# Six output buffers, a longer lag and kept-back product slots in the middle of a fused attention and two-layer kernel

## The chip, the cores and the metric

The kernel runs on one core of a Trainium2 chip. Times are device microseconds of one execution; a lower time is better. Each kernel is run several times, with the kernel before in the same rounds on the same chip. Faster or slower takes 2%.

## The reference

Attention of 4 batches x 8 heads x 768 positions x 64, where heads 0, 2 and 6 (the retrieval heads) see all earlier positions and the other five (the streaming heads) a window of 64 and the first four positions, the sinks; then a product with `w_in`, a leaky ReLU, and a product with `w_out`:

```python
scores = np.matmul(q, k.transpose(0, 1, 3, 2)) / sqrt(64)      # masked by head
a = softmax(scores)
x = np.matmul(a, v).transpose(0, 2, 1, 3).reshape(3072, 512)
h = x @ w_in                                                   # 512 x 2048
out = np.maximum(0.01 * h, h) @ w_out                          # 2048 x 512
```

## The kernel before

The 3072 rows are worked in eight chunks of 384. In the steady part TensorE works on three chunks at once: slots of the attention of chunk n+1, product slots (`in`) of chunk n, and sum slots (`out`) of chunk n-1, merged in program order. Every engine gets its instructions in that order; semaphores make them wait for one another. Heads are worked in four pairs, 0 to 3. Copying a result out of its PSUM bank is called its eviction; until then the next product into it waits (in the trace before, a `ph` eviction from 40.38 us ends at 40.87, and the weights of the next product start at 40.92). The kernel uses eight banks, two for each of four tags: `ph` (product), `psS` (scores, and transposes of the attention's result), `po` (values), `py` (sums).

```python
BANKS = {"ph": 2, "psS": 2, "po": 2, "py": 2}
...
k0, q0 = bf("k0", 3, H, D), bf("q0", 3, H, D)                  # memory of their own
f0 = {nm: rot.tile([128, DM], FP32, name="o", tag="o", bufs=3)... for nm in ("k", "q")}
...
def slots(self, order=range(H), lag=2):                        # one attention, in slots
    ...
    LAG, X = lag, 0 if self.cross else 3
    for t in range(len(units) + LAG + X):
        def slot(t=t):
            for p in range(4):
                if X and t == last[p] + LAG + X:
                    self.x_t(p, box[p], eng=self.xt_eng)       # transposes of pair p, into a psS bank
            if t < len(units):
                units[t][0]()                                  # scores into a psS bank, exp on ScalarE
            if 0 <= t - LAG < len(units):
                ... units[t - LAG][1]()                        # values, LAG slots later
                ... box[p] = self.finish(p)                    # reciprocal and scaling on VectorE
...
def in_slots(n, tags=("ph",)):       # 16 slots: 4 matmuls of 384 columns, eviction on ScalarE
...
            if hi == NG:             # end of a sum
                o = rot.tile([128, DM], FP32, name="o", tag="o", bufs=3)
                nc.vector.tensor_copy(o[:, 0 : c1 - c0], py[n][:, 0 : c1 - c0])
                nc.sync.dma_start(out=out[r0 : r0 + 128, c0:c1], in_=o[:, 0 : c1 - c0])
...
run(in_slots(1, ("ph",)))                                      # chunk 1's product, alone
...
run(merge(o0[10:] + o1[0:12], Attention(2).slots()))           # chunk 2's attention
run(spreads(3))
for n in range(2, NCH):
    ...
        extra = spreads(n + 2)                                 # key copies of chunk n+2, VectorE
    ...
        a = into(Attention(n + 1, cross=n > 2).slots(), extra)
    ms = merge(in_slots(n), outs)
    rest = ms[-9:] if a and n > 2 else []
    run(merge(ms[: len(ms) - len(rest)], a), rest)
```

The softmax here doesn't subtract the row's maximum and nothing guards it: scores larger than these inputs give would overflow.

## Time and profile before

| | before |
|---|---|
| median of three runs | 240.12 us (238.11 to 240.46) |
| span of the profiled run | 237.9 us |
| TensorE busy | 227.9 us, 96% |
| ScalarE / VectorE busy | 54% / 40% |

Shares of busy time do not say where time can be won, since a matmul's end in the profile is modelled: between 40 and 60 us TensorE shows 20.00 us busy of 20.00, with seven gaps of 0.09 us between starts in it (40.92 to 49.25 us). What is read below is when each matmul starts, against the start of the matmul before it plus the time that the columns of that earlier one take. The prediction shows the lines.

### The profile page before, as it was taken

What the parts mean: (1) busy time and instruction counts of PE and PEld (TensorE: products, weight loads), DVE (VectorE), ACT (ScalarE), POOL (GpSimd) and SP (SyncE); (2) the same over time, 40 slices, a digit from 0 to 9 for tenths busy, and PEclk for the clock granted to TensorE, in tenths of its full rate; (3) what the DMA queues carried; (4) which work ended last, traced back from release to release, by engine and by line L of the source; (5) the groups of instructions that cost most, each with busy time, mean ns of one, the idle gap of its engine ahead of it and who ended that gap; (6) DMA issues with size and microseconds to landing.
All of it is one profiled execution on the core that took longest, in us unless ns stands there. A gap on an engine that the chain in (4) does not pass through costs nothing.

```text
span 237.9 us, 5107 instructions
## 1 busy us (share of the span) xinstructions
PE 227.9 (96%) x2073; PEld 140.7 (59%) x2073; DVE 95.5 (40%) x281; ACT 128.4 (54%) x276; POOL 71.4 (30%) x87
## 2 busy tenths in 40 slices
PE   5889899999998999899999999999999999999995
PEld 3679666544665666466556565666556665555544
DVE  6587777105436345345512652144411441111112
ACT  4573875732663888664446543765556764333300
POOL 8975634035367087139002900000000000000000
PEclk9999999999999999999999999999999999999999
DMA  9999999999999999599929992930110211111012
GB/s 130 155 182 166 204 209 163 175 113 154 156 247 203 166 178 144 91 156 156 146 59 207 166 168 57 191 113 19 62 62 0 63 34 61 47 44 44 30 61 90
DMA packets 109480, 28.98 MB, mean 122 GB/s; under 512 B 101248, under 2 KB 105744, under 8 KB 109456
## 3 DMA queue, kind: packets, MB, share of 16 engines
q0 software_dynamic: 77088, 13.39, 74.2%
q1 hardware_dynamic: 31312, 15.00, 30.3%
q10 hardware_dynamic: 1056, 0.26, 0.5%
q8 instruction: 16, 0.26, 0.5%
q14 instruction: 8, 0.07, 0.1%
HBM read 27.30 MB, written 6.29 MB: 141 GB/s over the span
## 4 chain that ended last, share of the span: by engine, by line
PE 88%; DMA 4%; DVE 3%; ACT 3%; issue 1%; ACTq 0%; DVEq 0%
PE ph L553 32%; PE py L579 29%; PE po L294 6%; PE psS L325 5%; PE psS L579 3%; DMA out_dram<-o 3%; PE ph L566 2%; PE psS L360 2%; PE psS L305 2%; DMA o<-in_q_dram 2%; PE py L212 1%; ACT at L330 1%; PE psS L403 1%; PE po L510 1%; DVE xs L393 1%
## 5 line engine op out<-in xcount | busy, mean ns | idle before, releaser
L553 PE MATMUL ph<-xt,w_in_bf 128*128 128x384 bf16 x480 | 95.5, 325 | 0.0
L579 PE MATMUL py<-w_out_bf,g 128*128 128x512 bf16 (+1 forms) x352 | 91.0, 374 | 0.0
L555 ACT ACTIVATE g<-ph 128x384 bf16<-128x384 f32 x120 | 59.0, 492 | 57.5 <-PE ph L553 56.8
L553 PEld LDWEIGHTS <-w_in_bf 128*128 128x128 bf16 x480 | 43.7, 97 | 31.3 <-issue 1.3
L579 PEld LDWEIGHTS <-g 128*128 128x128 bf16 x416 | 35.7, 97 | 25.8
L330 ACT ACTIVATE at<-psS 128x384 bf16<-128x384 f32 x78 | 36.8, 490 | 15.5 <-PE psS L325 15.3
L585 DVE COPY o<-py 128x512 f32<-128x512 f32 (+1 forms) x22 | 14.9, 678 | 52.9 <-PE py L579 50.9
L112 POOL DMA_DIRECT2D kb<-in_k_dram x21 | 18.8, 908 | 38.3 <-DMA kd<-kb 37.8
L325 PE MATMUL psS<-qd,kt 128*128 128x384 bf16 (+2 forms) x90 | 22.9, 294 | 0.0
L117 POOL DMA_DIRECT2D va<-in_v_dram x24 | 21.3, 904 | 3.0 <-DMA w_out_bf<-in_moe_w_out_dram 1.5
L112 POOL DMA_DIRECT2D qb<-in_q_dram x21 | 18.7, 911 | 7.5 <-DMA w_in_bf<-in_moe_w_in_dram 3.2
L294 PE MATMUL po<-va,at 128*128 128x65 bf16 x228 | 19.4, 193 | 0.3 <-DVE at L333 0.3
L365 ACT ACTIVATE ats<-psS 128x384 bf16<-128x384 f32 x35 | 17.0, 490 | 4.4 <-PE psS L360 4.1
L369 DVE TENSOR_TENSOR ats<-ats,m_win 128x384 bf16<-128x384 bf16 x35 | 12.4, 358 | 16.3 <-ACT ats L365 16.2
L294 PEld LDWEIGHTS <-at 128*128 128x128 bf16 x234 | 15.1, 98 | 5.6 <-DVE at L333 0.7
L393 DVE TENSOR_TENSOR xs<-po,linv 128x384 bf16<-128x384 f32 x27 | 15.1, 558 | 0.9
L335 DVE TENSOR_TENSOR at<-at,m_caus 128x128 bf16<-128x128 bf16 x21 | 4.7, 226 | 24.9 <-ACT at L330 24.9
L360 PEld LDWEIGHTS <-kt 128*128 128x128 bf16 x210 | 10.8, 98 | 6.3 <-issue 0.4
L325 PEld LDWEIGHTS <-kt 128*128 128x128 bf16 x99 | 9.5, 97 | 7.6 <-issue 1.2
L294 PEld LDWEIGHTS <-ats 128*128 128x128 bf16 x210 | 10.1, 98 | 4.1 <-DVE ats L369 0.8
L233 DVE COPY kt<-kd 64x512 bf16<-64x512 bf16 x36 | 11.8, 326 | 0.6
L333 DVE TENSOR_TENSOR at<-at,m_caus 128x256 bf16<-128x256 bf16 x21 | 6.1, 293 | 14.6 <-ACT at L330 14.6
(139 smaller groups left out, 197.3 us busy)
## 6 DMA issues: line engine op xcount, KB each, us to landing
out_dram<-o SPq DMA_DIRECT2D x23, 256.0 KB, 2.3
va<-in_v_dram POOLq DMA_DIRECT2D x24, 128.0 KB, 7.5
kb<-in_k_dram POOLq DMA_DIRECT2D x21, 128.0 KB, 5.6
qb<-in_q_dram POOLq DMA_DIRECT2D x21, 128.0 KB, 5.9
w_in_bf<-in_moe_w_in_dram POOLq DMA_DIRECT2D x4, 512.0 KB, 10.1
w_out_bf<-in_moe_w_out_dram POOLq DMA_DIRECT2D x4, 512.0 KB, 12.7
vb<-va SPq DMA_DIRECT2D x8, 195.0 KB, 4.8
vb<-va SPq DMA_DIRECT2D x4, 130.0 KB, 3.1
```

The costliest lines, as they stand in the source:

```text
L112: nc.gpsimd.dma_start(out=t[:, g], in_=nat[nm][b, c, :, :, g])
L117: nc.gpsimd.dma_start(out=va[b][:, 3 * c + g, :, 0:D], in_=nat["v"][b, c, :, :, g])
L294: nc.tensor.matmul(o, lhsT=lhsT, rhs=rhs, start=first, stop=False, skip_group_check=True)
L325: nc.tensor.matmul(s[:, off : off + w], lhsT=kt[i][:, p, hh, 128 * kj : 128 * kj + 128], rhs=q_of(n, p, lo, CH), start=(j == 0), stop=(j = ...
L330: nc.scalar.activation(out=a[:, 0:off], in_=s[:, 0:off], func=ACTF.Exp, scale=SM)
L360: nc.tensor.matmul(s[:, 64 * m : 64 * m + 64], lhsT=kt[i][:, p, hh, k0 : k0 + 128], rhs=q_of(n, p, 64 * m, 64 * m + 64), start=(m == 0), s ...
L365: nc.scalar.activation(out=av_, in_=s[:, 0:CH].rearrange("p (j e f) -> p j e f", j=3, e=2), func=ACTF.Exp, scale=SM)
L393: nc.vector.tensor_tensor(xs[:], po[:, :, :, 0:D], linv.to_broadcast([128, 3, 2, D]), op=ALU.mult)
L553: nc.tensor.matmul(ph[:, 0:CH], lhsT=w_in_bf[:, g, 128 * t : 128 * t + 128], rhs=xts[n][:, g, :], start=(g == 0), stop=(g == KG - 1))
L555: nc.scalar.activation(out=gs[n][:, t, :], in_=ph[:, 0:CH], func=ACTF.Prelu, alpha=0.01)
L579: nc.tensor.matmul(py[n][:, 0 : c1 - c0], lhsT=gs[n][:, ng, 128 * tt : 128 * tt + 128], rhs=w_out_bf[:, ng, c0:c1], start=(ng == 0), stop= ...
L585: nc.vector.tensor_copy(o[:, 0 : c1 - c0], py[n][:, 0 : c1 - c0])
```

## The change

Its intent: the copy of a sum should not wait for an output transfer; the product that runs alone should borrow two idle banks; values should follow their scores three slots later; and the end of chunk 3's attention should have product slots to fill its waits, with the next key copies out of VectorE's way.

```diff
-    k0, q0 = bf("k0", 3, H, D), bf("q0", 3, H, D)
-    f0 = {... tag="o", bufs=3 ...}
+    k0 = rot.tile([128, 3, H, D], BF16, name="k0", tag="kd", bufs=2)
+    q0 = rot.tile([128, 3, H, D], BF16, name="q0", tag="qd", bufs=3)
+    f0 = {... tag="o", bufs=6 ...}
...
-                o = rot.tile([128, DM], FP32, name="o", tag="o", bufs=3)
+                o = rot.tile([128, DM], FP32, name="o", tag="o", bufs=6)
...
-    run(in_slots(1, ("ph",)))
+    run(in_slots(1, ("ph", "psS")))
...
-    run(merge(o0[10:] + o1[0:12], Attention(2).slots()))
+    run(merge(o0[10:] + o1[0:12], Attention(2).slots(lag=3)))
...
-            a = into(Attention(n + 1, cross=n > 2).slots(), extra)
+            a = Attention(n + 1, cross=n > 2).slots(lag=2 if n > 2 else 3)
+            a = into(a, extra) if n > 2 else a
...
+        if n == 2:
+            a, rest = a[:-3], [ms[-4], a[-3], ms[-3], a[-2], a[-1], ms[-2], ms[-1]] + extra
+            ms = ms[:-4] + rest
```

More of the change, by code (lines that the diff above doesn't have):

```diff
@@ L93 @@
     raw = {}
-    k0, q0 = bf("k0", 3, H, D), bf("q0", 3, H, D)
-    f0 = {nm: rot.tile([128, DM], FP32, name="o", tag="o", bufs=3).rearrange("p (h d) -> p h d", h=H) for nm in ("k", "q")}
+    k0 = rot.tile([128, 3, H, D], BF16, name="k0", tag="kd", bufs=2)
+    q0 = rot.tile([128, 3, H, D], BF16, name="q0", tag="qd", bufs=3)
+    f0 = {nm: rot.tile([128, DM], FP32, name="o", tag="o", bufs=6).rearrange("p (h d) -> p h d", h=H) for nm in ("k", "q")}
     def load_first(nm):
```

## The prediction

> **What bounds the kernel now.** I read the page first, then the waits, then the chain in order of time, and last the timeline of the stretch that the change touches (38 to 100 us).
>
> ```profile
> span 237.9 us, 5107 instructions
> PE 227.9 (96%) x2073; PEld 140.7 (59%) x2073; DVE 95.5 (40%) x281; ACT 128.4 (54%) x276; POOL 71.4 (30%) x87
> PE 88%; DMA 4%; DVE 3%; ACT 3%; issue 1%; ACTq 0%; DVEq 0%
> ```
>
> The chain in order of time has this line for the first product of chunk 1 (start, us, what):
>
> ```profile
> 38.30 11.76 PE ph L553 x68
> ```
>
> TensorE sets the end: 88% of the chain that ended last is its work. Only time in which TensorE could have started a matmul and did not is to be had. Its busy time does not show that, as ends are modelled; starts do. In the chain four 384-column matmuls take 0.65 us, 162 ns each. So I compare each matmul's start with the start before it plus its columns at 162 ns per 384 (30 ns for a 65-column one). Between 100 us and the last product this leaves nothing over 0.06 us but one 0.3 us gap at 170 us; 0 to 35 us has larger ones, which the change does not touch. What lies between 38 and 100 us is all that is on offer:
>
> 1. The chunk 1 first product, alone on TensorE: 68 matmuls at 162 ns are 11.02 us, the chain line has 11.76. The evictions show the pattern:
>
> ```profile
> 39.64 0.49 ACT L555 ACTIVATE g<-ph 128x384 bf16<-128x384 f32 x1 [0.16 <-PE ph L553]
> 40.38 0.49 ACT L555 ACTIVATE g<-ph 128x384 bf16<-128x384 f32 x1 [0.25 <-PE ph L553]
> ...
> 40.92 1.23 PEld L553 LDWEIGHTS <-w_in_bf 128*128 128x128 bf16 x8 [0.16 <-issue]
> 41.03 0.49 ACT L555 ACTIVATE g<-ph 128x384 bf16<-128x384 f32 x1 [0.16 <-PE ph L553]
> ```
>
> Evictions start 0.74 and 0.65 us apart in turn: two slots take 1.39 us where TensorE needs 1.30. The 40.38 eviction ends at 40.87, the next weights at 40.92: two ph banks are one too few. The stretch has seven such gaps of 0.09 us, 0.65 us in all.
>
> 2. Chunk 2's attention, 57 to 77 us:
>
> ```profile
> DVE o L585 <- DMA out_dram<-o: 1.6, 1, 1.6
> ```
>
> That was the line of the waits (who <- for whom: us, times, longest); in the timeline (start, us, what):
>
> ```profile
> 53.55 0.69 DVE L585 COPY o<-py 128x512 f32<-128x512 f32 x1 [10.55 <-PE py L579]
> ...
> 64.79 1.38 SPq L586 DMA_DIRECT2D out_dram<-o  x2
> ...
> 65.67 0.33 PE L360 MATMUL psS<-qd,kt 128*128 128x64 bf16 x6 [0.32 <-ACT xt L405]
> ...
> 71.06 0.69 DVE L585 COPY o<-py 128x512 f32<-128x512 f32 x1 [1.61 <-DMA out_dram<-o]
> ...
> 72.50 0.34 PE L403 MATMUL psS<-ident,xs 128*128 128x128 bf16 x3 [0.70 <-DVE xs L393]
> ...
> 74.90 0.20 PE L294 MATMUL po<-vb,ats 128*128 128x65 bf16 x1
> ```
>
> The sum copied at 53.55 is not sent until 64.79: the sync queue stood behind chunk 3's transposes. Three output buffers are then used up, the copy at 71.06 waits 1.61 us, reciprocal and scaling wait behind it, and TensorE's transposes come 0.87 us late (72.50, after a matmul that started at 71.54 and two of its kind). At 65.67 a score waits 0.49 us for the bank of a transpose that came just before it with no product between. At 74.90 the last streaming head's values wait 0.31 us for its mask.
>
> 3. Chunk 3's attention, 77.5 to 99 us: 0.13 us at 79.83, and at its end:
>
> ```profile
> 95.89 0.27 PE L294 MATMUL po<-va,at 128*128 128x65 bf16 x3 [0.29 <-DVE at L333]
> ...
> 96.72 0.24 PEld L294 LDWEIGHTS <-ats 128*128 128x128 bf16 x6 [0.30 <-DVE ats L369]
> ...
> 98.05 0.34 PE L403 MATMUL psS<-ident,xs 128*128 128x128 bf16 x3 [0.45 <-DVE xs L393]
> ```
>
> By starts: 0.45, 0.08 and 0.62 us. Sum of the stretch: 0.65 + (0.49 + 0.87 + 0.31) + (0.13 + 0.45 + 0.08 + 0.62) = 3.6 us, 1.5% of 240.12. That is the ceiling.
>
> [...]
>
> **The change part by part.**
>
> *Buffers.* k0 and q0 leave their own memory for the rotations of the transposed keys and queries: 2 x 3 x 8 x 64 x 2 bytes = 6 KB a partition, which pay for three more 2 KB output buffers. No added wait: k0 and q0 are long read when chunks 3 and 4 take their slots, and later chunks keep the same predecessors. With six buffers chunk 1's first sum no longer waits. The copy could start when VectorE is free at 69.45 and ends at 70.14, the last values of that pair start at 69.49, and their scaling would be done near 70.9, before the transposes' turn at about 71.63. Gain 0.87.
>
> *Four banks for the product of chunk 1.* Evictions of 0.49 us fit in 0.65 us slots. Gain 0.65.
>
> *Lag 3 and the product slots of chunk 2's attention.* It has 21 units; with lag 2 that is 26 slots over 18 product pieces, with lag 3 27 over 18. Laying the merge out by hand: the transposes of pair 0 now have a product piece behind them, so the 0.49 goes; the last streaming head has two pieces between score and values (about 1.5 us against the 1.2 it took from 73.58 + 0.16 to 74.90), so the 0.31 goes. But pair 2's transposes and the last streaming score now come right behind the last retrieval score: three takers of two psS banks with no product between. The score at 77.51 had its eviction from 77.87 to 78.36, so its bank is free 0.90 us after its start, while TensorE is at the next taker after 0.16 + 0.09 + 0.16 = 0.41. New wait 0.49. Net of this part 0.31.
>
> *Chunk 3's attention.* Again lag 3; the last four product pieces go around the last three slots. The 1.28 us of item 3 go: last values now have 1.3 us of product ahead of them, the last transposes 1.95. But 24 slots now share 16 pieces where 26 shared 20 (the eight key copies have no TensorE work). Here ScalarE evicts scores and products. Three slots and two products are 3 x 0.25 + 2 x 0.65 = 2.05 us of TensorE, and 5 x 0.39 = 1.95 us of ScalarE (two evictions back to back took 0.87, the second starting 0.38 after the first). It will run late: I put 0.2 us for the second of two scores behind pair 0's transposes, 0.2 for pair 2's transposes and 0.6 for the last streaming score, 1.0 in all. Net 0.3.
>
> *Key copies behind all.* Six copies took 1.84 us at 76.86 (0.31 each), two sink copies 0.17 and 0.15. They start after the copy of chunk 1's last sum: with T the end of that sum's matmuls, at T + 0.2 + 0.7. TensorE then has one product slot and three sum matmuls (1.30 us) before chunk 4's first score, which needs copy 1 (T + 1.2): just in time. The second score comes at T + 2.1 and needs copy 5, done at T + 0.9 + 1.53 = T + 2.43, about 2.5 with the signal. Loss 0.37.
>
> Sum: 0.87 + 0.65 + 0.31 + 0.3 - 0.37 = 1.75 us; 240.12 - 1.75 = 238.4.
>
> **Rivals.** (a) *Clean sweep:* psS waits don't arise, as ScalarE catches up in the sum pieces, and the key copies are in time: 3.5 us, 236.6. For it: ScalarE is 54% busy, and waits of 0.1 us need little to vanish. Against: the wait at 65.67 is the same three-takers pattern, there with lag 2. (b) *ScalarE becomes the bound* of chunk 3's stage: with 36 evictions in some 17 us every bank wait passes on, and 1 to 2 us more are lost: 239.9. Against: 36 x 0.39 = 14 us. (c) *The output wait hides another:* transfers (DMA share 1.90 between 60 and 80 us, more than full by the count of packet time) deliver chunk 4's or 5's loads no earlier, so time gained turns into load waits: about 239.5. Against: no DMA ends a TensorE wait in that stretch, and chunk 4's keys, loaded from 66.89, are not needed until 99. (d) *Chunk 4's key copies cost more:* its first four slots all wait, 1 us: 239.3.
>
> **Range and chances.** The ceiling is under 2%, so faster by over 2% needs chance in the runs (before spreads from 238.11 to 240.46). Slower by over 2% needs a stall of 6 us that nothing shows. 8 in 10: 236.6 (rival a) to 239.9 (rivals b, c). Chances 0.03, 0.95, 0.02.
>
> **What would show it.** Evictions of chunk 1's product 0.65 us apart throughout; no wait of a copy for an output transfer; no gap over 0.2 us between 64 and 77 us but one of 0.5 before the last streaming score; the same score in chunk 3's attention waiting 0.5 or more on an eviction; chunk 4's second score waiting for a key copy. I am wrong if chunk 3's stage (first product to first score of chunk 4) changes by over 1 us either way, or if anything after 105 us moves against its own start.

## The result, and the profile after

The changed kernel took 236.64 us in the median (236.42 to 237.29, six runs), the kernel before 240.03 (238.11 to 240.58, six runs). The ratio is 0.9876, 95% interval 0.9838 to 0.9914, so 1.2% less, within 2%. A ratio here is always the mean time of one kernel's fast runs over that of the other's of the same rounds, so it is not quite the ratio of the medians. From the page after (span; busy times; the chain by engine):

```profile
span 234.7 us, 5103 instructions
PE 225.8 (96%) x2073; PEld 139.9 (60%) x2073; DVE 97.6 (42%) x281; ACT 128.0 (55%) x276; POOL 71.3 (30%) x87
PE 91%; DVE 3%; ACT 3%; DMA 1%; issue 0%; DVEq 0%
```

The span fell by 3.25 us (237.92 to 234.67). To see where, I cut both traces at four starts of matmuls that both have: the first of chunk 1's product, the first score of chunk 2, the first of chunk 2's product, the first of chunk 3's product.

| stage, us | before | after | difference | predicted |
|---|---|---|---|---|
| start to chunk 1's product | 38.79 | 37.53 | -1.26 | 0 |
| to chunk 2's first score | 18.01 | 17.31 | -0.70 | -0.65 |
| chunk 2's attention, to chunk 2's product | 20.87 | 19.66 | -1.21 | -1.18 |
| chunk 3's attention, to chunk 3's product | 22.02 | 21.75 | -0.27 | -0.28 |
| to the end | 138.22 | 138.42 | +0.20 | +0.37 |

The four stages that the change touches lose 1.98 us, against 1.74 in the prediction's sum (which rounds some terms, 1.75). The first stage, where only the place of two tiles changed, loses another 1.26.

Chunk 1's product, in the chain in order of time (start, us, what): `ph` and `psS` in turn, 0.65 us apart, with nothing between.

```profile
38.34 0.65 PE psS L554 x4
38.99 0.65 PE ph L554 x4
39.64 0.65 PE psS L554 x4
```

Chunk 2's attention, from the timeline after (start, us, engine, line, operation, out<-in, count, idle time before and what ended it):

```profile
66.71 0.69 DVE L586 COPY o<-py 128x512 f32<-128x512 f32 x1
...
69.08 0.33 PE L326 MATMUL psS<-qd,kt 128*128 128x256 bf16 x2
...
69.34 0.33 PE L404 MATMUL psS<-ident,xs 128*128 128x128 bf16 x3
69.45 0.49 ACT L331 ACTIVATE at<-psS 128x384 bf16<-128x384 f32 x1 [0.19 <-PE psS L326]
...
69.99 0.34 PE L361 MATMUL psS<-qd,kt 128*128 128x64 bf16 x6 [0.32 <-ACT at L331]
```

The copy of chunk 1's first sum, which had waited 1.61 us for an output transfer, no longer waits, and the transposes at 69.34 come in their turn. Right behind them the last streaming score (69.99) waits for the eviction that ends at 69.94: the score at 69.08, the transposes and this score are three takers of two banks. Transposes are three matmuls of 128 columns, 0.16 us by starts (68.02 to 68.18 in the same trace); the start comes 0.49 us after that.

Chunk 3's attention, and the start of chunk 4's, from the same view:

```profile
89.58 0.33 PE L404 MATMUL psS<-ident,xs 128*128 128x128 bf16 x3
...
90.35 0.33 PE L361 MATMUL psS<-qd,kt 128*128 128x64 bf16 x6 [0.44 <-ACT at L331]
...
97.19 0.10 PEld L326 LDWEIGHTS <-kt 128*128 128x128 bf16 x1 [0.35 <-DVE kt L234]
```

The same three takers, and here ScalarE also has a product to evict between (at 89.40, 0.51 us): 0.60 us before 90.35 by starts (89.58 + 0.16 to 90.35), and 0.13 before the transposes. The second score of chunk 4 waits for a key copy; by starts that is 0.19 us.

The first stage differs in how fast TensorE runs. Four matmuls of 128 columns, in the timeline before and after:

```profile
11.82 0.62 PE L212 MATMUL py<-ident,k 128*128 128x128 bf16 x4
...
13.03 0.39 PE L212 MATMUL py<-ident,q 128*128 128x128 bf16 x4
```

```profile
9.03 0.63 PE L213 MATMUL py<-ident,q 128*128 128x128 bf16 x4
...
10.97 0.39 PE L213 MATMUL py<-ident,k 128*128 128x128 bf16 x4
```

They start about 107 ns apart in the lines of 0.62 and 0.63, 56 ns apart in those of 0.39. The clock records of the two traces set in at 12.70 us before and at 10.17 us after. An estimate from these numbers: 2.53 us more at about half speed (107 against 56 ns) cost at most 1.27 us where TensorE always has work; the stage lost 1.26. Whether the change moved that moment, or the run did, this pair cannot tell.

### The profile page after: what moved, and what is told of

Same layout as the page of the kernel before. It is cut to its first block, busy times and chain, and to the rows that moved or that the text cites.

```text
span 234.7 us, 5103 instructions
## 1 busy us (share of the span) xinstructions
PE 225.8 (96%) x2073; PEld 139.9 (60%) x2073; DVE 97.6 (42%) x281; ACT 128.0 (55%) x276; POOL 71.3 (30%) x87
## 4 chain that ended last, share of the span: by engine, by line
PE 91%; DVE 3%; ACT 3%; DMA 1%; issue 0%; DVEq 0%
PE py L580 32%; PE ph L554 30%; PE po L295 6%; PE psS L326 5%; PE psS L580 3%; PE psS L361 3%; PE ph L567 2%; PE psS L554 2%; PE psS L306 2%; DMA o<-in_k_dram 1%; ACT at L331 1%; PE py L213 1%; PE psS L404 1%; ACT g L556 1%; PE po L511 1%; DVE qt L188 1%
## 5 line engine op out<-in xcount | busy, mean ns | idle before, releaser
L554 PE MATMUL ph<-xt,w_in_bf 128*128 128x384 bf16 x448 | 90.5, 326 | 0.0
L556 ACT ACTIVATE g<-ph 128x384 bf16<-128x384 f32 x112 | 55.0, 492 | 56.6 <-PE ph L554 55.9
L234 DVE COPY kt<-kd 64x512 bf16<-64x512 bf16 x36 | 12.8, 355 | 0.6
L392 DVE RECIPROCAL linv<-po 128x6 f32<-128x6 f32 x27 | 5.2, 193 | 15.2 <-PE po L295 15.2
```

The costliest lines, as they stand in the source:

```text
L554: nc.tensor.matmul(ph[:, 0:CH], lhsT=w_in_bf[:, g, 128 * t : 128 * t + 128], rhs=xts[n][:, g, :], start=(g == 0), stop=(g == KG - 1))
L556: nc.scalar.activation(out=gs[n][:, t, :], in_=ph[:, 0:CH], func=ACTF.Prelu, alpha=0.01)
```

## The experiments

Theory: the four stages gain what waits they lose (2.0 us), and the 1.26 us of the start are of the run. Rivals: the new place of the first keys and queries moved the start; or a single part, the lag or the kept-back slots, carries the gain. Twelve kernels were run, in three groups (after_again, u_ph, u_bufs, u_lag; before_again, b_move, b_bufs, u_tail; the last four), each group on one chip with 11 runs of the kernel before. All gave right results. The traces of these twelve miss 26 to 28 matmul records each, many of which show as a gap of 0.215 us, one 512-column matmul, before a sum; those are not counted. Stages are cut as in the table above.

**after_again: the changed kernel, unaltered.**

> The changed kernel itself, unaltered. Waits between 38 and 100 us as in its first trace: sum of start gaps over 0.045 us about 1.9 us, the largest the last streaming score of chunk 2 (0.49) and of chunk 3 (0.60). Theory chance: the moment at which TensorE goes from 107 to 56 ns between 128-column matmuls (12.5 us in the trace before, 10.2 us in the one after) is of the run, so it may fall elsewhere this time[...]. Theory layout (moving the first keys and queries into the rotations makes TensorE fast earlier): 10.2 us again.

236.62 us (236.16 to 237.44), ratio 0.9873 (0.9828 to 0.9918). Stages 17.39, 19.67, 21.76, 138.43: the middle repeats within 0.08 us, 0.09 us of it a wait for chunk 2's queries before its first score. The start did not repeat: the clock record has full speed from 4.05 us, half from 7.46, full from 10.88. That speaks for chance: in this trace the changes are 3.41 and 3.42 us apart, and in the first one the step was at another place in the kernel, at 10.17 us.

**before_again: the kernel before, unaltered.**

> The kernel before itself, unaltered. Waits between 38 and 100 us as in its first trace (3.6 us). Theory chance: the moment of TensorE's full speed falls [...]not at 12.5 us again. Theory layout: 12.5 us again. The ratio to the kernel before must be 1.000 within its interval; its width is the noise of all the others.

238.46 us (238.12 to 239.12), ratio 0.9995 (0.9974 to 1.0016). Full speed at 11.66 us in place of 12.70, and the first stage 38.31 in place of 38.79. Stages 18.02, 20.72, 22.02, 138.22. The same kernel thus moves its own start by half a microsecond. Its level also differs between chips: in the three groups its 11 runs had medians of 240.14, 238.74 and 238.97, but lowest runs of 238.20, 238.19 and 238.01.

**b_move: before, with the first keys and queries in the rotations.**

```diff
-    k0, q0 = bf("k0", 3, H, D), bf("q0", 3, H, D)
+    k0 = rot.tile([128, 3, H, D], BF16, name="k0", tag="kd", bufs=2)
+    q0 = rot.tile([128, 3, H, D], BF16, name="q0", tag="qd", bufs=3)
```

> The kernel before with only the first keys and queries moved into the rotations. No wait between 38 and 100 us changes. Theory layout: TensorE is at full speed near 10.2 us and the time falls by 1.3 us. Theory chance: same time as before, ratio 1.000 within 0.003.

239.36 us, ratio 1.0028 (1.0003 to 1.0053): no gain; if anything a little longer. The trace had full speed at 9.14 us, the times did not follow it. A gain of 1.3 us from the move is excluded. t_both below has the moved tiles too, and its trace had full speed only at 12.15 us. The traces alone would leave it open that the move made the start earlier: without added empty matmuls, eight of the nine with moved tiles begin chunk 1's product at 37.34 to 37.68 us, and the two of the kernel before at 38.31 and 38.79. b_move's profiled run was the fastest of its six.

**u_ph: the changed kernel, chunk 1's product on two banks.**

```diff
-    run(in_slots(1, ("ph", "psS")))
+    run(in_slots(1, ("ph",)))
```

> Product of chunk 1 on its own two banks again, all else as changed. Both theories of the start: seven gaps of 0.09 us back between the evictions, starts 0.74 and 0.65 us apart in turn; span between the first slot of that product and its first sum 0.65 us longer; nothing else moves. Time +0.65 us on the changed kernel (0.3%).

237.45 us, 0.8 more in the median than after_again of the same rounds. The stage is 18.02 us, 0.63 more than the 17.39 of after_again, with the gaps of 0.09 back. (0.09 of the 17.39 was a wait for queries, so the gaps cost 0.72.) "Nothing else moves" missed: the rest is 0.47 longer, since a value of chunk 4 waited 0.46 us for its mask; in this trace VectorE's work at that place met a GpSimd operation (see u_lag).

**u_bufs: the changed kernel with three output buffers.**

```diff
-... name="o", tag="o", bufs=6
+... name="o", tag="o", bufs=3
```

> Three output buffers again, first keys and queries still in the rotations. The wait of the copy of chunk 1's first sum for the first output transfer comes back. Theory A (it costs what it cost before): 0.87 us. Theory B (lag 3 left less room behind it: the copy could start at 66.7 and must wait until about 71, then reciprocal and scaling, so pair 2's transposes move from 69.3 to some 72.3): 2 to 3 us. On the start of the kernel: theory layout says fast from 10.2 us as in the changed kernel, theory chance says anything.

239.30 us (237.26 to 240.56), 2.7 more in the median than after_again. Timeline:

```profile
66.03 1.84 SPq L587 DMA_DIRECT2D out_dram<-o  x2
...
70.40 0.69 DVE L586 COPY o<-py 128x512 f32<-128x512 f32 x1 [3.78 <-DMA out_dram<-o]
...
71.85 0.34 PE L404 MATMUL psS<-ident,xs 128*128 128x128 bf16 x3 [2.36 <-DVE xs L394]
```

Theory B holds: the copy waits 3.78 us, the transposes come 2.5 us late, and the stage is 21.71 us against 19.67. It is not 2.5 more because the wait at the last streaming score vanishes in it. So the buffers are worth 2.0 us in that stage of the changed kernel, not 0.87. The last stage is 0.63 longer as well, where VectorE's key copies met GpSimd's multiplication (2.50 us for six, see u_lag), so the 2.7 in the time is not the buffers' wait alone.

**b_bufs: before, with six output buffers** (and the move).

> The kernel before with six output buffers (and the move that pays for them). The copy of chunk 1's first sum no longer waits for an output transfer, pair 2's transposes of chunk 2 come 0.87 us earlier: -0.9 us, 0.35%. Rival: something else (a load, a bank) holds the transposes up as long: under 0.3 us.

238.37 us, ratio 0.9994 (0.9971 to 1.0017): no gain in the time. The wait for the transfer is gone from the trace, but:

```profile
55.96 0.34 PE L326 MATMUL psS<-qd,kt 128*128 128x384 bf16 x1 [0.36 <-DMA qd<-qb]
...
70.79 0.33 PE L404 MATMUL psS<-ident,xs 128*128 128x128 bf16 x3
70.90 0.49 ACT L331 ACTIVATE at<-psS 128x384 bf16<-128x384 f32 x1 [0.19 <-PE psS L326]
...
71.44 0.33 PE L326 MATMUL psS<-qd,kt 128*128 128x256 bf16 x2 [0.32 <-ACT at L331]
```

With the transposes in time, the score behind them waits 0.49 us for a bank. In the kernel before the longer wait covers it. The stage is 20.47 us, 0.40 less than before's 20.87 (0.25 less than before_again's). The stage ahead of it is 0.5 longer, since chunk 2's queries had not landed: that ate the rest, in this run. My theory said 0.9, the rival under 0.3; the rival was right on the time, and named the bank, though it holds up the next score and not the transposes.

**u_lag: the changed kernel with lag 2.**

```diff
-    ... Attention(2).slots(lag=3)        ...slots(lag=2 if n > 2 else 3)
+    ... Attention(2).slots(lag=2)        ...slots(lag=2)
```

> Lag 2 again in chunks 2 and 3, all else as changed. Chunk 2's attention: 0.49 us before the first streaming score of pair 1 and 0.31 us before the last values come back, the 0.49 us before the last streaming score goes: +0.3 us. Chunk 3's: the merge no longer puts pair 2's transposes and the last streaming score behind one another, so 0.13 + 0.60 go, but the last values wait some 0.4 us: -0.3 us or more. Together within 0.5 us of the changed kernel. Rival, that lag 3 is what made the gain: +1 us or more.

238.65 us, 2.0 more in the median than after_again; the rival was right. Chunk 2's stage is 20.47 (+0.8): the two waits that I named, and pair 2's transposes stand between two scores with no product here too, which I had overlooked. Chunk 3's is 22.90 (+1.1), with the same 0.13 + 0.60, 0.31 for the last values, and one I had not thought of:

```profile
85.61 0.93 POOL L128 TENSOR_TENSOR vs<-vsf,m_sink 32x448 bf16<-32x448 f32 x1 [7.25 <-PE psS L361]
85.64 1.05 DVE L334 TENSOR_TENSOR at<-at,m_caus 128x256 bf16<-128x256 bf16 x1 [1.06 <-ACT at L331]
```

A mask that takes 0.29 us elsewhere took 1.05 beside GpSimd's multiplication, and the values behind it came 0.91 us late. The key copies fit that: six took 1.86 us in the changed kernel's first trace, where that multiplication came after them (98.19), and 2.50 in u_bufs, where it ran from 98.44 beside them; there chunk 4's second score waited 0.82 us, not 0.19. In u_lag's own trace the six took 2.48 and that score waited 0.81. No run takes that multiplication away, so that it is what slows VectorE there is the author's reading of these meetings. With lag 3 a mask has a slot more to be late in. This trace is 2.98 us longer than that of after_again: 0.80 in chunk 2's stage is the order; the mask's 0.91 in chunk 3's and 0.62 at the end are the meetings with GpSimd; 0.39 is a later landing of chunk 2's queries. Whether the other five runs met GpSimd in the same way is not known, so the 2.0 us in the time is not all shown to be the lag's.

**u_tail: the changed kernel without the tail** (key copies among the attention, nothing kept back, lag 3).

```diff
-            a = into(a, extra) if n > 2 else a
+            a = into(a, extra)
...
-        if n == 2:
-            ...
```

> The changed kernel with chunk 4's key copies among chunk 3's attention again and no product slots kept back, lag 3 kept. Theory (the tail of the change is a loss): 0.13 + 0.60 + 0.18 us of bank waits and 0.19 us of waits for key copies go, since a product piece stands between the last scores; the last transposes wait 0.6 us for their scaling again, as before: -0.5 us on the changed kernel. Rival (the tail is what the change gains in this stage): +0.6 us or more.

236.94 us, ratio 0.9923 (0.9900 to 0.9946) on its chip. Chunk 3's stage is 22.36 us, 0.61 more than in the changed kernel, and the rest 0.19 less: the tail is worth 0.42 us in the traces, so the rival had the stage, though not the whole. The last transposes wait 0.62 us as I said, but 0.40 before other transposes and 0.25 for a mask come to it, and the 0.18 after pair 0's transposes stays. This is read from traces alone: the changed kernel did not run in these rounds.

**t_both: two further moves.** Pair 2's transposes one slot later, and the key copies ahead of the last two product slots:

```diff
+            XP = {p: X + (p == 2 and lag == 3) for p in range(4)}
-                    if X and t == last[p] + LAG + X:
+                    if X and t == last[p] + LAG + XP[p]:
...
-... a[-2], a[-1], ms[-2], ms[-1]] + extra
+... a[-2], a[-1]] + extra + [ms[-2], ms[-1]]
```

> The changed kernel with two further moves: pair 2's transposes one slot later (so that they no longer stand between the last two scores without a product), and chunk 4's key copies ahead of the last two product slots. Bank theory: 0.49 us before the last streaming score of chunk 2, 0.13 + 0.60 before that of chunk 3 and 0.19 before chunk 4's second score go, up to 0.2 stays where the last streaming score waits for the score two before it: -1.2 us on the changed kernel, stage of chunk 2's attention 19.2 us in place of 19.66, stage of chunk 3's 21.0 in place of 21.75, rest 138.2 in place of 138.4. Rival (ScalarE as a whole is what limits chunk 3's stage): the waits move on to other scores and its stage stays at 21.5 or more.

235.38 us (234.50 to 236.35), ratio 0.9845 (0.9808 to 0.9882). Stages 17.31, 19.18, 21.22, 138.23: the bank theory's numbers within 0.2 us. In sum 1.2 us less than the changed kernel from chunk 1's product on, though this run had full speed only at 12.15 us and the first stage took 38.48.

**t_warm and b_warm: nine more empty matmuls in the start**, in the changed kernel and in the kernel before.

```diff
-    idle("psS", 13)
+    idle("psS", 19)
     turn_tile("k", 0, "va")
     turn_tile("q", 0, "v")
+    idle("psS", 3)
```

> The changed kernel with nine more empty matmuls in the start, where TensorE would be idle[...]. Theory phase: full speed from 7 us or before in the trace, product of chunk 1 begins up to 1 us earlier (36.5 to 37.5). Theory load: chunk 2's first score then waits for its transposed queries, which land at 54.9 to 56 us in all traces so far, so the stage from product 1 to it grows by as much and the time stays within 0.3 us of the changed kernel. Rival: the whole 1 us shows in the time.

> The same nine empty matmuls in the kernel before. If the start's phase is what the changed kernel's profile gained beyond the waits (1.26 of its 3.2 us), the kernel before with a settled start gets near its own fastest runs, 238.1 to 238.3 in the median, with less spread, and the changed kernel with the same start is 1.7 to 2.0 us faster than this one, the sum of the waits. If instead the change moved the start, the difference stays at 3 us.

Both traces have full speed early, from 4.72 and 6.11 us, and chunk 1's product starts at 36.11 and 36.29. In t_warm

```profile
5.34 0.40 PE L213 MATMUL py<-ident,k 128*128 128x128 bf16 x4 [0.26 <-DVE k L665]
```

is already a fast group. t_warm took 236.37 us (235.03 to 237.00), ratio 0.9874; b_warm 238.25 (median of all six), ratio 0.9953 (0.9914 to 0.9992; two slow runs, 241.71 and 242.26, left out). With the nine matmuls in both, the means of the fast runs are 236.15 (six) and 238.04 us (four), 1.9 us apart where the kernels without them are 3.0 to 3.1 apart. That is near the 1.98 of the first pair's four stages, but this pair's own traces do not show it: their spans differ by 3.13 us and their four stages by 2.95, since in b_warm chunk 2's stage is longer (below) and t_warm's profiled run is its fastest. So 1.9 us is what the times say here, and that it is the sum of the four stages is not shown.

The load theory failed in t_warm's trace: chunk 2's queries were there at 53.42, and the whole gain of the start is in its span (233.3). But that was the fastest of its runs; the mean is no better than the changed kernel's ratio. What the other runs lost, no trace shows.

In b_warm the gain of the start is partly given back:

```profile
64.42 1.00 SPq L586 DMA_DIRECT2D out_dram<-o  x2
...
69.53 0.69 DVE L585 COPY o<-py 128x512 f32<-128x512 f32 x1 [2.59 <-DMA out_dram<-o]
...
70.98 0.34 PE L403 MATMUL psS<-ident,xs 128*128 128x128 bf16 x3 [1.69 <-DVE xs L393]
```

Chunk 2's attention starts 2.5 us earlier than in before's first trace (54.30 against 56.80), yet the sync queue sends the first output at 64.42, against 64.79: it stands behind chunk 3's transposes (58.41 and 61.02 there), and in before's trace those had waited 3.7 and 1.9 us for that chunk's loads. The stage takes 21.85 us, 0.98 more than before.

**t_both_warm: all of these.**

> Both of these at once: two moves and nine empty matmuls. As the two moves alone if chunk 2's queries bound the start (within 0.3 us); faster by up to 1 us if they do not.

234.44 us (233.97 to 234.70, five runs), ratio 0.9807 (0.9769 to 0.9845), span 232.2. That is 1.0 us less in the mean than t_both of the same rounds, and 4.6 less than before. It is faster than the kernel before; whether by 2% is unclear, as the interval has 0.98 in it. The changed kernel itself did not run in these rounds; t_warm did, at 236.15 in the mean.

## Why the prediction was right or wrong

The measured 236.64 us is inside the range of 236.6 to 239.9, by 0.04 us, and the class (within 2%) is right. The point of 238.4 was 1.8 us too high. The signs that it named all came: evictions 0.65 us apart, no wait of a copy for an output transfer, waits of 0.49 and 0.60 at the two last streaming scores, a wait of chunk 4's second score for a key copy. That the range held is in part luck: some 2.0 of the 3.4 us between the medians are waits of the kind that it reckoned with, and the rest is not.

*The waits of the sum.* Product of chunk 1: 0.65 predicted, 0.70 in the trace, 0.63 undone by u_ph. The prediction counted seven gaps; the trace before has eight (before the starts at 39.53, 40.92, 42.31, 43.70, 45.09, 46.48, 47.86 and 49.25), 0.73 in all, and the 68 matmuls of its chain line take in the last four of chunk 0. So its ceiling was 3.7 us. The new wait at chunk 2's last streaming score: 0.49 predicted, and found in five traces (after, after_again, u_ph, u_tail, t_warm). Chunk 3's stage: 0.2, 0.2 and 0.6 predicted, 0.18, 0.13 and 0.60 measured, plus 0.15 and 0.10 at places I did not name; net 0.27 against 0.28. Key copies: 0.37 predicted, 0.19 in the two traces of the changed kernel, but 0.81 and 0.82 where GpSimd's multiplication met them. Sum 1.75 predicted, 1.98 by stages in the first pair.

*The term that was mis-sized* is "Gain 0.87" for the buffers. I had taken the gap that the trace showed as what the buffers give, alone and in any order. Alone they gave 0.40 us in the stage and nothing in the time (b_bufs), since a bank wait hid behind the wait for the transfer. In the changed order they give 2.0 us (u_bufs), since the transfer lands at its own time and a faster order only waits longer for it (the copy starts at 70.40 in u_bufs after 3.78 us of waiting, at 71.06 in the kernel before after 1.61). Chunk 2's stage by lag and buffers: 20.87 us with lag 2 and three, 20.47 with lag 2 and six (b_bufs), 21.71 with lag 3 and three (u_bufs), 19.66 with lag 3 and six; each is of one trace, and u_lag, with lag 2 and six, has 20.47 again. So lag 3 is worth 0.81 us with six buffers, where 0.31 was predicted, and costs 0.84 with three. The two errors, 0.47 too much for the buffers and 0.50 too little for the lag, cancelled by luck: 1.18 predicted, 1.21 measured. The parts of this change do not add up one by one.

*What the sum left out* is the start: -1.26 us in the profiled pair. I had written that 0 to 35 us is not touched. The place of two tiles was, but the times show no gain from it (b_move; t_both with the same tiles was late again), and unaltered kernels move their own start by run. The traces lean to the move all the same (see b_move), so the cause of this part stays open. What sets the moment of full speed is not shown. In the traces without added empty matmuls the clock record had full speed to stay from 9.14 us (b_move) to 12.70 (before), and the first stage took 37.34 to 38.79 us, 1.45 us apart in a kernel of 238; after_again and b_bufs had full speed before that too, from 4.05 and 4.03, and lost it after 3.41 us (b_bufs: full at 4.03, half at 7.44, full at 10.85). With nine more empty matmuls it came at 4.72 (t_warm) and 6.11 (b_warm). The times' 3.0 to 3.5 us between the kernels (by means or medians) are more than the stages' 1.98, and the lowest runs differ by less (238.11 against 236.42, 238.20 against 236.16: 1.7 and 2.0). On the chip of the first group the kernels with three buffers spread over 3.5 us (before) and 3.3 (u_bufs), those with six over 1.3, 1.7 and 1.9 (11 runs of before, six of each other). That the buffers cut off slow runs, in which the transfer lands later, fits this and b_warm; it is argued, as no trace of such a slow run was taken, and before_again on another chip spread over 1.0 alone.

*The rivals.* (a), the clean sweep at 236.6, came near the time but not for its reason: its psS waits did arise. (b) ScalarE as the bound did not come; t_both took its waits away by order alone. (c) Chunk 2's queries took time back in b_bufs (0.52), u_lag (0.47), u_tail (0.28) and after_again (0.09), not in the profiled run; loads of chunks 4 and 5, which the rival named, did not. (d) was 0.19, or 0.82 with GpSimd. In the two traces of the changed kernel nothing after chunk 4's start moved by more than 0.2, as foreseen.

## What to carry to other kernels

When two waits stand one behind the other, the visible gap of the first is not what its removal gives (here 0.87 us removed gave 0.40 in its stage, b_bufs): look for the next taker of each bank and buffer in the new order, by hand, before adding up. With few buffers a copy can be bound to a transfer that sits behind unrelated transfers in the sync engine's program order (the sum copied at 53.55 us was sent at 64.79, and a later copy waited 1.61 us for it), and then a faster start or order is eaten there (b_warm: 2.5 us earlier moved the sending by 0.4; u_bufs: the copy waits 3.78 us); three more buffers took that wait away. What this gains depends on the order: here nothing in the time for the kernel before, 2.0 us in one stage of the changed one. Cut traces into stages at instructions that both kernels have, so that a clock step (here at 12.70 and 10.17 us) or a load at the start isn't taken for the change.
